# A shorter exponent table, parameter products from PSUM, and a new written-out order in an S4D and gMLP kernel

## The chip, the cores and the metric

The kernel runs on one core of a Trainium2 chip. Its engines are TensorE (PE, with its weight loads shown apart as PEld), VectorE (DVE), ScalarE (ACT), GpSimd (POOL) and SyncE (SP, which here only issues DMAs). Each has its own in-order queue; they meet through semaphores. The metric is the device time of one execution in microseconds, lower is better; the median of several runs counts.

## What is computed

The reference, cut to what matters. `A_u` is 2048 x 512, there are 128 modes for each of the 512 channels, and the mixer is 1792 wide.

```python
def _A_ref(u, log_A_real, A_imag, C_real, C_imag, log_dt, D_skip):
    dt = jnp.exp(log_dt)
    A = -jnp.exp(log_A_real) + 1j * A_imag
    C = (C_real + 1j * C_imag) * dt[:, None]
    P = jnp.exp((A * dt[:, None])[:, :, None] * pos[None, None, :])
    K = 2.0 * jnp.einsum("dn,dnl->dl", C, P).real
    y = jnp.fft.irfft(jnp.fft.rfft(u_t, L2) * jnp.fft.rfft(K, L2)[None], L2)[:, :, :L]
    return y + u * D_skip[None, None, :]
def _B_ref(x, w_in, w_sp, b_sp, w_out):
    z = _gelu(jnp.einsum("bsd,df->bsf", x, w_in))
    z1 = z[..., :Fh]
    z2 = _layernorm(z[..., Fh:], axis=-1)
    g = jnp.einsum("ts,bsf->btf", w_sp, z2) + b_sp[None, :, None]
    return jnp.einsum("bsf,fd->bsd", z1 * g, w_out)
h = x + _A_ref(_layernorm(x, axis=-1), ...)
h2 = h + _B_ref(_layernorm(h, axis=-1), ...)
```

## The kernel before

**Phase A** (`phase_a`, line 268) makes the long convolution. The channels are cut into 4 chunks of 8 units each. A unit (`unit`, line 483) builds a piece of the kernel K: its exponentials come from a table `mt` of short rows of powers, which `table` (line 473) makes once for each half chunk, eight tables in all. POOL multiplies the rates by the list `c_lt` in three instructions, ACT takes one Exp over the whole table, and POOL multiplies the weights into the last four columns. Each unit then makes three 128x512 factors by POOL, each the product of eight entries of one part of the row with four of another (lines 498 to 501); ACT makes sines from phases in PSUM, DVE multiplies, and TensorE contracts.

`params` (line 405) turns the complex weights C into modulus, phase and real part, for chunk 0, chunk 1, and chunks 2 and 3 together. Its last steps multiply the sine and cosine of an angle (`si`, `co`) by the smaller and the larger part (`mn`, `mx`) and add them, on POOL (lines 459 to 461), before ACT, TensorE and a copy bring the result to `rcs`, which the table's last multiply reads. `norm_x` (line 366) normalises x ahead of its transform: DVE takes statistics and writes part of the result, and 64 column scalings fill the rest, each on ACT or on POOL.

The transforms are pieces: A and B for x, C and D for K, E for the inverse. D multiplies the two spectra; in the last chunk three of its eight groups go through an ACT copy and two POOL multiplies each (lines 608 to 612) and the others through one DVE multiply. `piece_e` writes `big`, from which the next phase reads.

All of phase A is first recorded and then issued in an order that is written out by hand, as three strings. `RANKS` (line 37) holds a rank for each recorded operation, two digits each: the sorted ranks are the order on all five queues. `FORMS` says for each choice (`either`) which engine takes it: evacuations of PSUM on ACT or DVE, column scalings on ACT or POOL. `BANKS` gives each PSUM tile one of five banks. The instructions of this phase all carry line 252, the line that issues them.

**Phase B1** (`phase_b1`, line 700) finishes the inverse and makes z1. `lines(n, g, g+1)` (line 748) is TensorE's last stage for a quarter n of the positions, into PSUM tiles `y`, of which there are seven. `put_by` (line 764) copies a tile to `stash` by two ACT copies of 64 partitions, `add` (line 770) adds x to it on DVE, `moments` takes its statistics and stores h, `centre` forms the mean over partitions by TensorE (`lnh_pm`) and the squares, `spread` does the same for the variance (`lnh_pv`), and `root` takes the inverse root. `by_halves` and `transposed` scale, transpose and split the result into two parts `ht`, and `column` multiplies it by the weights (`pz`), takes the gelu on ACT and stores z1. The order is that of the calls from line 889 on, on every engine but SP.

**Phases B2 and B3** make z2, the spatial product and the output projection; they are not touched.

Of the kernel before, what the change touches and what calls it, by code (L numbers as in the profile page):

```python
# [23 lines left out]
NCH = 4  # L24
# [47 lines left out]
def constants():  # L72
# [40 lines left out]
    for i in range(8):  # L113
# [12 lines left out]
    c["c_lt"] = np.broadcast_to(-lt, (P, 34))  # L126
# [141 lines left out]
def phase_a(ctx, gen, tc, ins, cst, ident, c_mean, c_inv, Q, wp, scr):  # L268
# [8 lines left out]
    def one(pool, tag, shape, dt=F32):  # L277
        return pool.tile([P] + shape, dt, tag=tag, name=tag)
# [9 lines left out]
    c_lt, c_f, dpad, half_pi, magic, dummy, dts, ndt, dt2 = (wb(n) for n in (34, 256, P, 1, 1, 1, NCH, NCH, NCH))  # L288
# [3 lines left out]
    mts = [one(g1, f"mt{h}", [64, 34]) for h in range(2)]  # L292
# [112 lines left out]
    def params(al, c0, n, rt):  # L405
# [13 lines left out]
        si = ai  # L419
# [19 lines left out]
        nc.scalar.activation(co, a, AF.Sin, bias=half_pi)  # L439
# [260 lines left out]
def phase_b1(tc, es, right, left, rest, c_mean, mhalf, qt, ins, cst, wp, scr):  # L700
# [69 lines left out]
    def add(n, g):  # L770
        v = xqs[n % 3][:, 4 * g:4 * g + 4, :]
        nc.vector.tensor_add(v, stash[n][:, g].rearrange("p (l x) -> p l x", l=4), v)  # L772
# [114 lines left out]
    with tc.manual_schedule(engines={E.PE, E.DVE, E.Activation, E.Pool}):  # L887
# [7 lines left out]
        nc.scalar.activation(stats[:, 1, 0, 0:1], mhalf, AF.Gelu_apprx_tanh)
# [400 lines left out]
```

## Time and profile before

| | |
|---|---|
| median of 3 runs | 819.7 us (815.72 to 820.77) |
| profiled execution | 819.86 us, its span 818.1 us |
| TensorE busy | 766.9 us, 94% of the span |
| DVE, ACT, POOL busy | 592.3, 456.3 and 308.5 us |
| mean granted TensorE clock | 0.992 |
| phase A, to the first `y` matmul | 274.87 us |
| first `pz` matmul of z1 | 297.28 us |

A row of the view by groups reads: line, engine, operation, output <- inputs, shapes, count, then busy time and mean time of one in ns, then the idle time of the engine just before these instructions and what ended most of it. A row of the timeline reads: start, length, engine, line, operation, names, shapes, count, and in brackets the idle time before it and what ended it. A row of the view by stretches gives the stretch, then the busy time and number of instructions of PE, PEld, DVE, ACT and POOL, the granted clock, the share of the DMA engines, and GB/s.

### The profile page before, as it was taken

What the parts mean: (1) busy time and instruction counts of PE and PEld (TensorE: products, weight loads), DVE (VectorE), ACT (ScalarE), POOL (GpSimd) and SP (SyncE); (2) the same over time, 40 slices, a digit from 0 to 9 for tenths busy, and PEclk for the clock granted to TensorE, in tenths of its full rate; (3) what the DMA queues carried; (4) which work ended last, traced back from release to release, by engine and by line L of the source; (5) the groups of instructions that cost most, each with busy time, mean ns of one, the idle gap of its engine ahead of it and who ended that gap; (6) DMA issues with size and microseconds to landing.
All of it is one profiled execution on the core that took longest, in us unless ns stands there. A gap on an engine that the chain in (4) does not pass through costs nothing.

```text
span 818.1 us, 20010 instructions
## 1 busy us (share of the span) xinstructions
PE 766.9 (94%) x8081; PEld 652.2 (80%) x8081; DVE 592.3 (72%) x1153; ACT 456.3 (56%) x813; POOL 308.5 (38%) x356
## 2 busy tenths in 40 slices
PE   2489999999988889999999999999999999999998
PEld 1267889889978787888999888888888888888887
DVE  8998987967763468642677799978849883887534
ACT  8999989788653575553233355575345442454111
POOL 8999999978456100000331101233220002231200
PEclk9999999999998999999999999999999999999999
DMA  7604514415049146552361146999798449799642
GB/s 262 205 14 154 119 51 108 102 51 115 2 106 397 63 104 169 143 192 97 96 139 49 65 122 173 204 225 237 180 229 203 151 124 190 165 252 249 140 114 79
DMA packets 65004, 119.48 MB, mean 146 GB/s; under 512 B 6800, under 2 KB 21264, under 8 KB 63632
## 3 DMA queue, kind: packets, MB, share of 16 engines
q1 hardware_dynamic: 53248, 96.71, 39.5%
q0 software_dynamic: 11664, 21.50, 15.8%
q8 instruction: 63, 1.03, 0.5%
q14 instruction: 29, 0.24, 0.1%
HBM read 90.40 MB, written 19.40 MB: 134 GB/s over the span
## 4 chain that ended last, share of the span: by engine, by line
PE 61%; DVE 1%; ACT 1%; issue 0%
PE m L1183 34%; PE pz L978 9%; PE pz L876 8%; PE po L1106 7%; PE pl L1106 2%; DVE stats L776 0%; ACT ht L833 0%; ACT w1r L824 0%; DVE w1r L831 0%; DVE xq L772 0%; ACT stash L768 0%; DVE ht L837 0%; PE lnh_pm L785 0%; PE lnh_pv L799 0%; ACT zo L879 0%
## 5 line engine op out<-in xcount | busy, mean ns | idle before, releaser
L1183 PE MATMUL m<-wts,zc_wa 128*128 128x512 f32 x700 | 221.0, 395 | 0.0
L1183 PEld LDWEIGHTS m<-wts,zc_wa 128*128 128x128 f32 x700 | 131.7, 188 | 31.0
L1054 POOL DMA_DIRECT2D raws<-in_w_sp_dram x64 | 58.2, 1016 | 213.4 <-DMA raws<-in_w_sp_dram 206.3
L1183 PE MATMUL m<-wts,zc_wb 128*128 128x512 f32 x350 | 138.0, 394 | 0.0
L252 POOL TENSOR_TENSOR wa<-mt 128x512 f32<-128x512 f32 x96 | 106.7, 1130 | 12.1 <-DVE big L252 4.2
L690 ACT CAST wts<-raws 128x512 fp32r<-128x512 f32 x112 | 69.1, 619 | 51.3 <-PE m L1183 26.2
L691 DVE TENSOR_TENSOR wts<-raws,wts 128x512 fp32r<-128x512 f32 x112 | 76.4, 685 | 15.5 <-ACT wts L690 15.5
L1183 PEld LDWEIGHTS m<-wts,zc_wb 128*128 128x128 f32 x350 | 65.8, 188 | 15.6
L978 PE MATMUL pz<-w,ht 128*128 128x448 f32 x384 | 77.0, 362 | 0.0
L876 PE MATMUL pz<-ht,w1h 128*128 128x512 f32 (+1 forms) x248 | 73.8, 377 | 2.9 <-ACT ht L833 2.6
L978 PEld LDWEIGHTS pz<-w,ht 128*128 128x128 f32 x384 | 72.0, 188 | 4.9
L984 POOL TENSOR_SCALAR sm<-sm 128x1 f32<-128x1 f32 x16 | 5.6, 347 | 165.0 <-DVE sm L983 165.0
L252 PE MATMUL ps<-c_inv,trio 128*128 128x128 f32 x512 | 60.8, 277 | 1.9 <-DVE trio L252 1.4
L1106 PE MATMUL po<-w,gz 128*128 128x512 f32 x252 | 61.7, 392 | 0.0
L252 PEld LDWEIGHTS ps<-c_inv,trio 128*128 128x128 f32 x512 | 58.5, 192 | 3.3 <-POOL trio L252 1.6
L690 ACT CAST zc_wa<-raws 128x384 fp32r<-128x384 f32 (+1 forms) x70 | 37.1, 533 | 41.5 <-DVE raws L1088 21.5
L252 PE MATMUL ps<-big,a 128*128 128x128 f32 x448 | 57.4, 285 | 1.2 <-ACT big L252 0.7
L252 DVE TENSOR_TENSOR f<-ps,wa 128x512 f32<-128x512 f32 (+1 forms) x64 | 46.9, 750 | 14.2 <-ACT ps L252 12.5
L252 PEld LDWEIGHTS ps<-big,a 128*128 128x128 f32 x448 | 53.8, 197 | 3.7 <-DVE trio L252 0.9
L1106 PEld LDWEIGHTS po<-w,gz 128*128 128x128 f32 x252 | 47.3, 188 | 10.7
L876 PEld LDWEIGHTS pz<-ht,w1h 128*128 128x128 f32 x248 | 45.1, 188 | 12.8 <-ACT ht L833 3.5
L690 ACT CAST zc_wa<-z 128x128 fp32r<-128x128 f32 (+2 forms) x56 | 23.7, 431 | 45.6 <-PE m L1183 38.7
(157 smaller groups left out, 1463.0 us busy)
## 6 DMA issues: line engine op xcount, KB each, us to landing
raws<-in_w_sp_dram SPq DMA_DIRECT2D x112, 256.0 KB, 4.1
raws<-in_w_sp_dram POOLq DMA_DIRECT2D x80, 256.0 KB, 6.0
trio<-trio SPq DMA_DIRECT2D x32, 256.0 KB, 4.3
scr_z<-zo SPq DMA_DIRECT2D x28, 256.0 KB, 2.1
big<-in_u_a_dram SPq DMA_DIRECT2D x8, 512.0 KB, 6.1
xq<-in_u_b_dram SPq DMA_DIRECT2D x4, 1024.0 KB, 9.0
g<-in_c_g_dram SPq DMA_DIRECT2D x4, 1024.0 KB, 9.1
scr_h<-xq SPq DMA_DIRECT2D x16, 256.0 KB, 4.1
```

The lines of the kernel that those rows point to most:

```text
L252: r = getattr(getattr(self.nc, e), method)(*map(self.real, args), **{k: self.real(x) for k, x in kw.items()})
L690: nc.scalar.copy(hi, src)
L691: (engine or nc.vector).tensor_tensor(lo, src, hi.bitcast(F32), op=ALU.subtract)
L876: nc.tensor.matmul(pt[:, w], a[:, q, f], ht[n][k][:, q, w], start=((q, i) == terms[0]), stop=((q, i) == terms[-1]))
L978: nc.tensor.matmul(pt[:, :FQ], a[:, q], w2[:, b, q, f], start=(q == 0 and i == 0), stop=(q == 3 and i == 2))
L984: nc.gpsimd.tensor_scalar_add(sm[:, 14:15], sm[:, 13:14], 1e-5)
L1054: nc.gpsimd.dma_start(r, ws[1], accum_op=ALU.add)
L1106: nc.tensor.matmul(pt, gz[fb][x][:, P * a:P * a + P], wo[:, y, fb, w], start=(first and fb == fbs[0] and i == 0), stop=(last and fb == fbs ...
L1183: nc.tensor.matmul(pt, x[:, f], y, start=(k == 0 and i == 0), stop=(k == KT - 1 and i == 2))
```

## The change

The list behind the table has 27 entries for 34: the part that held 7 to 0 is gone, and the unit reads the part 0 to 7 backwards in its place; 0 to 448 by steps of 64 is one part of eight. In `params`, `si` and the cosine `cp` are PSUM tiles, and DVE makes their products and the sum; six more PSUM tiles are to be placed. All three strings are new. Between the inverse and z1, the first two groups of quarter 0 are not put by: DVE adds them to x straight from PSUM, in two halves each. The adds and statistics go in pairs, `lines(2, 0, 1)` stands before `centre(0)`, and the root of quarter 0 before `lines(2, 2, 3)`.

```diff
     lt = np.concatenate([
-        24 - 8 * np.arange(4), 1 + np.arange(7), 7 - np.arange(8), 64 * (1 + np.arange(7)),
-        32 + 8 * np.arange(4), 512 * np.arange(4),
+        24 - 8 * np.arange(4), 1 + np.arange(7), 64 * np.arange(8), 32 + 8 * np.arange(4), 512 * np.arange(4),
     ]).astype(f8)
...
-        si = ai
+        si, cp = bank("si", [P, N]), bank("co", [P, N])
...
-        nc.scalar.activation(co, a, AF.Sin, bias=half_pi)
+        nc.scalar.activation(cp, a, AF.Sin, bias=half_pi)
...
-        nc.gpsimd.tensor_tensor(co, co, mx, op=ALU.mult)
-        nc.gpsimd.tensor_tensor(si, si, mn, op=ALU.mult)
-        nc.gpsimd.tensor_tensor(co, co, si, op=ALU.add)
+        nc.vector.tensor_mul(co, cp, mx)
+        nc.vector.tensor_mul(si, si, mn)
+        nc.vector.tensor_add(co, si, co)
...
-        nc.gpsimd.tensor_tensor(mv[:, :, :, 30:], mv[:, :, :, 30:], w.unsqueeze(3).to_broadcast([P, 8, 8, 4]), op=ALU.mult)
+        nc.gpsimd.tensor_tensor(mv[:, :, :, 23:], mv[:, :, :, 23:], w.unsqueeze(3).to_broadcast([P, 8, 8, 4]), op=ALU.mult)
...
-        for i, (a0, b0) in ((2, (18, 30)), (0, (3, 26)), (1, (11, 0))):
-            ta = mt[:, d0:d0 + 16, a0:a0 + 8].unsqueeze(2).to_broadcast([P, 16, 4, 8])
+        for i, (a, b0) in ((2, (slice(11, 19), 23)), (0, (slice(3, 11), 19)), (1, (slice(10, 2, -1), 0))):
+            ta = mt[:, d0:d0 + 16, a].unsqueeze(2).to_broadcast([P, 16, 4, 8])
...
     def add(n, g):
         v = xqs[n % 3][:, 4 * g:4 * g + 4, :]
-        nc.vector.tensor_add(v, stash[n][:, g].rearrange("p (l x) -> p l x", l=4), v)
+        if n == 0 and g < 2:
+            y = ys[n, g].rearrange("p l (x d) -> p l d x", d=4)
+            v = xqs[0][64 * g:64 * g + 64, :8].rearrange("p l (d x) -> p l d x", d=4)
+            for odd in range(2):
+                nc.vector.tensor_add(v[:, odd::2], y[64 * odd:64 * odd + 64], v[:, odd::2])
+        else:
+            nc.vector.tensor_add(v, stash[n][:, g].rearrange("p (l x) -> p l x", l=4), v)
...
-        for n in range(2):
-            for g in range(4):
-                put_by(n, g)
+        put_by(0, 2)
+        put_by(0, 3)
+        for g in range(4):
+            put_by(1, g)
         nc.scalar.activation(stats[:, 1, 0, 0:1], mhalf, AF.Gelu_apprx_tanh)
-        for g in range(4):
+        for g in range(0, 4, 2):
             add(0, g)
+            add(0, g + 1)
             moments(0, g)
+            moments(0, g + 1)
+        lines(2, 0, 1)
         centre(0)
-        lines(2, 0, 1)
         add(1, 0)
+        root(0, spread(0))
         lines(2, 2, 3)
-        root(0, spread(0))
         put_by(2, 0)
         put_by(2, 1)
```

The three strings differ in nearly every entry and are left out here; what they say of the order is told where it is used.

More of the change, by code (lines that the diff above doesn't have):

```diff
@@ L58 @@
-    "JeI4I6IMI1I2IIIcI3IJI5ILINIWIdIfIzI-JIJXI+J4JFJ5J7J8JRJPJJJQJLJMJNJSJTJUJYJZJaIOIiInI8IgIhIwIqJAJ0J1J6JBJCJDJEJKJbJcJuJw"
-    "JfJgJhJrJkJpJjJmJqJnJiJoJlJxJ+JzJyJ-JsJtKCKEK2K9K6KFK3KAK0K1K7K8K4K5KBKD"
+    "01000H0g290N0Z181A1P1a1k1l1h470+6W0a02030B270k2g060708090A0C0E0F0I0P0R0U0b0i0G0l1J0u1C0J1213151E1F1K0D0L0K0Q0S0V0T0d0e0f"
+    "0m0n0-16171G1T1U1j1V1b1Q1S1m1s1t1v0t0h0y1X1u1w0M05040O0o1W0z0r0p2D101R2C2A1M110q2H2e4V5P2o1H2q464N0j0c0X0Y0w0x0W1r0s1B1x"
+    "1-1D140v1I1y1i1+1q1N1L191p1c1f1O1n1d1g2120222E2G2J2K2V2L2M2W2Y2d2h2i2s2v2x2y2+3134333v3f3w3W3T3k3y4E3t3K3L433x3E4W3J3j3l"
@@ new lines @@
+    "623I4Q3G4C3b6C353R5J404B593F4D3B382O24373Y263P2B2t393S3O323Q2F2R3C282P2N2p2Q3e2U3H2n3N2a2-2c3d2X363g3h3i3m3r4T3s3u3-4448"
+    "4H4J4L4R4X4Z4d4h4o4i4p4s534q4w644v5E4t5b5s685x506j5+5z6z5r5-5A5S6S5p5H6f6r5O5Y5C6y54716s6l7G757i7zAN1Y1Z1o2Z2l2m2u3M1e1z"
+    "23252I2SGn2T2f2b2z3A3n3p4I4O4Y4u5D2r4-4a5V6J6Y6n8P2w3D3c4r5F5W4F4x4e4c5T5U606k6t5i5k5j5l5m5nHS696M6F6O6g6o6p6+6-707H7J7o"
+    "AZ7v907n8IAgB6BJBg6G6N6b7g8d8gB3CpCq61635R5X6H6I5f5g6K6L5G5Q5o5q5y666m6u898A7l807O7c6q736X6a7m866d6e8i8r304M2j3V3z45494A"
@@ new lines @@
+    "4g4b4y4l4z52878o8q3Z3U2k3X3a3o3q414G424S4K4U4f888J8K4P51564j4k4+5Z5a5d5c655e6A6D6T7p7q3+4m4n5557585B5K5M5L5h5N5u5w7T8z92"
+    "7I817f5I7a7s8H6777795t5v6E6x76787A7M7P7X7b9M9U9V6R6Z6B6P6Q6c6U6V6i6h6w6v7D7E7Q8+8-7k8F7y7+7-858C8D8G8E8U8S8m8s8t9J9K7Y7K"
+    "7N7L7Z7j7F7R7U7S8M7V8N8O999I9LAE8l7r9dA4A6AI8Q8R7W7d7t7u7w7x7e7h727483847B7C8e8f9495ATAU9l9o8p8v9z9+AXAh9N9P9mA59Y9g9u9v"
+    "AJAKAOAPACADAbAn9-A3C7CRBTBdCMCcBRBSCoCrBWBxAuAyAwB5DLDM8L978n8j8k8x988y919R9C969O9D9W9f9nBuC88Z8X8V828B8T8u8b8a8c8Y8W93"
@@ new lines @@
+    "8w9A9E9wAlAq9Z9h9q9Q9c9i9p9x9r9y9k9sA1A2A9AACXD0D28h9B9S9F9G9H9T9j9e9t9X9aA09bA7ABBCBmBtBaBPBLBnBUBvB-AdALAVAFAGAHBAAMAi"
+    "AfAQAWB4BKBMBNCEDUDfAmAzA8AjAkArB1AvAsB7A-AtB0B2B8BEBlChCiA+BZBjBIBVBcBzC9BpCFBiBkCJCACPCdCfD1D4BDBOBYBFBGBHBXBqBeByBQBb"
+    "BfBhC1C2CeCyCzCjC3CgDQDtDuENASAYAaARAeAcAoApB9AxBBBrBoBwCWBsB+CBCvCwE0CCCDDxDGDHDeDjDADBE8EBDbDcDVDoE9EEDEDFDqDsEUEaDgDr"
+    "DhDyE7EFEcEdEGEYE6ECGRGWFVFWGUGfEwE+GQGXFUFhFiFqFIFJGVHcCGCVCQCZCaCbClC-CmD7CnCkD8C+DJDKEhFbFxC0C4C5C6CHCICNCSCLCTCOCKCU"
@@ new lines @@
+    "CYCtCxDSFYFZDCDPDTDNDODXDkDYDiDwDlDmDnDpDzD+D-ESEeCsCuDID3D5D6DDDRD9DWDZDaDvDdE1E2FpGdGmFXFaEXF1EDFSFTEOELEAE3E4E5EHEVEP"
+    "ElEMEIEkEWEmEoG3H8HOEZEtEiEbEfEgF0ExEpEyEuEqF6F3FCFDFyG4GDEsEvFKF2F5F7FeFAFBFsF8FMFrFkFzF-GbHCHDE-FFFPF4FGFHFvFRFLFlFNFQ"
+    "FuFwG8G9GFGeGtHAGgHdGxGMHgH+EJEQEKERETEjF9FOFEEnErEzFfFgFnFcFoFdGiGjG0G1HEHLHxHyGuGvHsHtHFHVHGHeI6IDGwH5HzI4HmHwHkHlHoHv"
+    "H-I8HnHuHPHfHbHrIMIQI9IEIOIdIiInIAIBILIRIqIyIPIfJYJZFtF+G7FjG2G5GSGNGAGOG6GCGcGTGkGlIsIxJ4FmGBGEGGGHGIGaGKGJGLGYGPG-GhH2"
@@ L60 @@
+    "H4J5J6J7GZGpGoGqGrGsH6H7GzHNG+GyHMHBHWHpHqJNJOH0H9H3H1HHHIHXHTHKHUHQHJHRHYHZHaI3J9JAI0HiHjI5ICIFIZISIHITINIGIWIaIbIuIzI+"
+    "J8IIHhIJI1I2I7IcIgIKImIXIUIYIhItJPJVJWJXIVIvIpIeIjIkI-IoIlJ1IwIrJBJ0JKJLJdJeJfJDJIJEJ2J3JCJHJQJFJRJJJGJSJMJTJUJaJbJcJnJo"
+    "JgJhJrJiJsJtJlJmJyJ-JpJqJjJkJ+JzJwJxJuJvK8KAK3K9K2KBK6K7KEKFKCKDK4K5K0K1"
 )
 FORMS = (
-    "000000001010100011000011100100000101100000011000001000000111001100110000100000000000100111100001010101101111101000000001"
-    "00000110110110010100000100100100001110010100000010000001000110001101001101100000000101101110001001100000111001101111"
+    "000000000011100110101010101011010000101001001000110111001101001110100011101000001000011000100100010100000100011111000000"
@@ L64 @@
+    "00000011010001000101110111101011100100000101010101011010010101111101001000010010001010101000011001110100000001101011"
 )
 BANKS = (
-    "414220313014444030432220022044434342124120412142014001422000123112321121011031223434430243400423134324420430131103321432"
-    "034214411300222000123324434132420203334344321432242224410132113203001432002102101211314313432104023143234243141003422442"
-    "030104322301034014314303413333144024"
+    "421123440400211334443433310202101124431134224211421042214022402042214110302201001124433033402433414403033414410430132223"
@@ L69 @@
+    "011421213103311240021020111332040242104433432434432340214123210331143003421331224020021220434431434211300343212301113104"
+    "411340232010300042233021313434433404313424"
 )
@@ L287, in phase_a @@
     cs_bufs = [wb(2 * W).rearrange("p (k a w) -> p k a w", k=2, a=2) for _ in range(2)]
-    c_lt, c_f, dpad, half_pi, magic, dummy, dts, ndt, dt2 = (wb(n) for n in (34, 256, P, 1, 1, 1, NCH, NCH, NCH))
+    c_lt, c_f, dpad, half_pi, magic, dummy, dts, ndt, dt2 = (wb(n) for n in (27, 256, P, 1, 1, 1, NCH, NCH, NCH))
     c_k = one(g1, "c_k", [2, W], F32R)
@@ L291, in phase_a @@
     sws = [one(g1, f"sw{h}", [4, 2, NS]) for h in range(2)]
-    mts = [one(g1, f"mt{h}", [64, 34]) for h in range(2)]
+    mts = [one(g1, f"mt{h}", [64, 27]) for h in range(2)]
     f_bufs = [one(g1, f"f{i}", [4, W]) for i in range(3)]
```

26 lines of the change are left out of this document (3 added, 23 removed).

## The prediction

> **What bounds the kernel now.** I read first the chain of work that ended last, then the time by stretches, then the groups of instructions by shape, and last the timeline at three places that the change touches.
>
> ```profile
> 321.49 5.38 PE pz L876 x22
> ```
>
> The columns are start, length and what ran. From here on the chain has nothing but TensorE until the last 4 us or so: whatever the change saves must be saved before that, and is then kept to the end.
>
> ```profile
> 0.00:40.00 40.00, 12.99 (x94) 8.63 (x95) 35.12 (x152) 35.58 (x83) 36.25 (x47) 1.00 0.73 239
> 40.00:80.00 40.00, 34.45 (x1045) 27.02 (x1045) 35.49 (x49) 38.50 (x71) 38.64 (x48) 1.00 0.27 86
> 80.00:160.00 80.00, 78.49 (x1935) 70.01 (x1938) 68.51 (x91) 73.17 (x106) 78.00 (x81) 1.00 0.41 97
> 160.00:240.00 80.00, 78.52 (x1780) 71.91 (x1773) 56.30 (x73) 59.32 (x81) 55.17 (x60) 1.00 0.25 57
> 240.00:275.00 35.00, 29.74 (x388) 28.52 (x392) 13.90 (x17) 8.94 (x14) 16.71 (x12) 0.85 0.72 264
> 275.00:300.00 25.00, 20.16 (x543) 19.20 (x543) 13.81 (x48) 18.23 (x32) 0.00 (x0) 0.93 0.35 87
> ```
>
> The columns after the stretch are PE, weight loads, DVE, ACT, POOL, the granted clock. Up to 40 us PE is starved and the three others are about 90% busy. From 40 to 160 us POOL is 97% busy (116.64 of 120 us) and ACT 93%; from 160 to 240 us POOL and ACT have some 20 us to spare and PE is the bound. From 240 to 300 us every engine has gaps: that is the tail of the transforms and the way to the first z1 product, and there a wait is worth its full length.
>
> **The change, part by part.**
>
> ```profile
> L252 POOL TENSOR_TENSOR mt<-wb 128x816 f32<-128x816 f32 x16 | 25.6, 1606 | 1.4 <-ACT trio L252 1.3
> L252 POOL TENSOR_TENSOR mt<-wb 128x544 f32<-128x544 f32 x8 | 9.0, 1130 | 0.0
> L252 ACT ACTIVATE mt<-mt 128x2176 f32<-128x2176 f32 x8 | 16.0, 2017 | 0.1
> L252 ACT ACT_TABLE_LOAD x16 | 20.5, 1283 | 2.7 <-PE ps L252 1.1 <-PEq L1290 0.7 <-DVE big L252 0.7
> L252 POOL TENSOR_TENSOR trio<-trio 128x128 f32<-128x128 f32 x12 | 5.3, 451 | 0.3
> L252 POOL TENSOR_TENSOR big<-big 128x256 f32<-128x256 f32 x6 | 4.2, 704 | 0.4 <-ACT big L252 0.4
> L252 DVE TENSOR_TENSOR trio<-trio,ps 128x128 f32<-128x128 f32 x2 | 0.6, 284 | 0.0
> L252 POOL TENSOR_TENSOR wa<-mt 128x512 f32<-128x512 f32 x96 | 106.7, 1130 | 12.1 <-DVE big L252 4.2 <-ACT mt L252 3.9 <-PE ps L252 2.3
> L252 DVE TENSOR_TENSOR trio<-ps,trio 128x1024 f32<-128x1024 f32 x29 | 34.2, 1217 | 7.4 <-PE ps L252 6.9
> L252 DVE TENSOR_TENSOR f<-ps,wa 128x512 f32<-128x512 f32 x56 | 37.4, 684 | 11.2 <-ACT ps L252 9.5 <-POOL ks L252 1.3 <-POOL wa L252 0.2
> ```
>
> *Table of 27.* Each of 8 tables is three POOL multiplies and one Exp. POOL's two shapes give (1606-1130)/272 = 1.75 ns an element; 448 elements fewer are 0.78 us a table, 6.3 us in all. Exp by proportion (2017 x 7/34) saves 0.4 us each, 3.3 us.
>
> *Falling powers read backwards.* One of a unit's three 128x512 multiplies reads its short factor with a negative step. No row has one. The 96 of a unit take 1130 ns with their several strides; two plain POOL operands take 451 and 704 ns for 128 and 256 elements, which would be 1210 ns for 512. So between -2.6 and +2.6 us for 32 of them (0.08 us each way); I take 0, by the 96, which are this instruction. POOL being the bound up to 160 us, either end would show.
>
> *Parameter products from PSUM.* Nine multiplies and adds leave POOL: 6 x 0.451 + 3 x 0.704 = 4.8 us. On DVE they are 6 x 0.284 + 3 x about 0.42 (my estimate, scaled by the step from 128 to 256 elements that POOL shows) = 3.0 us, in stretches where DVE is 88% busy.
>
> *New order.* The three strings give each engine's order outright, so I compared the two orders entry by entry. Of the free choices, nine column scalings go from ACT to POOL, the net of the PSUM evacuations moves four 128x512 copies from ACT to DVE, and two 128x256 copies go back to ACT.
>
> ```profile
> 0.73 3.90 POOL L252 MEMSET sw<- 32x1024 f32 x4 [0.29 <-POOLq L1290]
> 5.91 4.24 POOL L252 TENSOR_TENSOR mt<-wb 128x816 f32<-128x816 f32 x3 [1.27 <-ACT trio L252]
> 7.43 0.26 ACT L252 ACTIVATE ps<-ps 128x128 f32<-128x128 f32 x1 [0.24 <-DVE ps L252]
> 7.71 1.28 ACT L252 ACT_TABLE_LOAD   x1
> 9.00 0.37 ACT L252 ACTIVATE trio<-ps,wb 128x128 f32<-128x128 f32 x1
> 23.94 2.34 ACT L252 ACTIVATE big<-big,trio 128x96 f32<-128x96 f32 x6
> 28.90 3.48 POOL L252 TENSOR_SCALAR big<-big,trio 128x96 f32<-128x96 f32 x5
> ```
>
> A column scaling costs ACT 2.34/6 = 0.39 us and POOL 3.48/5 = 0.70 us: +6.3 us for POOL, -3.5 us for ACT. POOL's sum is -6.3 - 4.8 + 6.3 = -4.8 us; DVE's is +3.0 and four copies of about 0.68 less two small ones, +5 us.
>
> Table loads: I counted switches between the function sets of Exp, Arctan and Sin along ACT's order. A dummy Sin now stands ahead of the first Arctan, which saves one; tables 0.0 and 0.1, and 2.0 and 2.1, no longer share an Exp stretch, which adds four: 19 for 16, +3 x 1.283 = +3.8 us. ACT's sum is -3.3 + 3.8 - 3.5 and about -2 for copies, -5 us. A load is followed at once by the next activation (7.71 + 1.28, then 9.00). The Trainium skill, ScalarE: Activation LUTs, What ACT_TABLE_LOAD costs, adds some 1380 ns of drain to each switch; by it three loads would be 8.0 us and ACT's sum near -1, but the rows here show no drain.
>
> The start speaks against the change. POOL now multiplies its first table at 5.91 us with 2.0 us idle before. In the new order the copy of the rates that it waits for stands on ACT behind the table load for Sin, Arctan, two Sines and an Abs; SP also issues the list for the table behind two blocks of u and c_inv. From 7.43 us, four 0.3 us steps and the copy put that start near 8.9 us, with only two memsets (1.95 us) ahead: 6.9 us idle, 4.9 more. Against POOL's -4.8 that is nothing saved by the end of the stream, and by units 18 and 19, where POOL's sum is only 4.0 less, 0.9 lost. I take +0.5 us for everything up to 240 us; between -4.8 (the idle start is covered) and the price of the slow rival below. SP's other moves (stack loads earlier, later block loads) feed work that is behind POOL's queue here. What is queued on DVE behind the nine new operations is the x normalisation, which feeds the first transforms; I hold that to be inside the 0.5.
>
> ```profile
> 248.20 8.24 PE L252 MATMUL ps<-big,a 128*128 128x128 f32 x56 [0.70 <-ACT big L252]
> 253.57 6.20 POOL L252 TENSOR_TENSOR trio<-trio 128x512 f32<-128x512 f32 x5 [1.28 <-ACT trio L252]
> 259.50 14.65 PE L252 MATMUL ps<-c_inv,trio 128*128 128x128 f32 x128 [1.41 <-DVE trio L252]
> ```
>
> *Last spectrum product (D3).* Three of its eight groups go by an ACT copy to six POOL multiplies of 1.24 us. Now the second copy comes after another group, and POOL waits 1.28 us. In the new order the three copied groups come first, so the six run without that wait. DVE is last next: its first group is there after four of PE (8 matmuls each, 14.65/128 = 0.114 us apart, 3.7 us), and five products of 1.22 us end at 9.8 us, where the inverse now starts 11.3 us after the first matmul: -1.5 us. Bounds: 0 (only two banks alternate now, and the waits stay) to -2.2 (POOL alone sets it: 0.9 for PE, 0.8 for a copy of the 0.6 us kind and its hand-over, 6 x 1.24, so 9.1).
>
> ```profile
> 274.87 7.57 PE L756 MATMUL y<-big,g 64*64 64x128 f32 x256 [0.72 <-ACT big L252]
> 277.00 9.55 ACT L768 COPY stash<-y 64x512 f32<-64x512 f32 x16 [2.18 <-PE y L756]
> 279.40 0.69 DVE L772 TENSOR_TENSOR xq<-stash,xq 128x512 f32<-128x512 f32 x1 [5.65 <-ACT stash L768]
> 280.13 0.87 DVE L776 BATCH_NORM_STATS2 stats<-xq 128x6 f32<-128x128 f32 x4
> 285.55 0.68 PE L785 MATMUL lnh_pm<-stats,c_mean 128*128 128x16 f32 x4 [3.11 <-DVE stats L776]
> 286.15 5.28 PE L756 MATMUL y<-big,g 64*64 64x128 f32 x128
> 286.57 1.28 ACT L895 ACT_TABLE_LOAD   x1
> 291.36 0.62 PE L799 MATMUL lnh_pv<-small,c_mean 128*128 128x16 f32 x4
> 291.91 3.72 PE L756 MATMUL y<-big,g 64*64 64x128 f32 x128
> 292.02 0.17 DVE L804 TENSOR_SCALAR small<-lnh_pv 128x16 f32<-128x16 f32 x1 [4.39 <-PE lnh_pv L799]
> 294.00 1.37 DVE L822 TENSOR_SCALAR w1r<-xq,small 128x128 f32<-128x128 f32 x5
> 297.28 0.39 PE L876 MATMUL pz<-ht,w1h 128*128 128x256 f32 x1 [1.65 <-ACT ht L833]
> ```
>
> *Between inverse and z1*, against the same start at 274.87. DVE is idle twice: 5.65 us for ACT's copies, and 4.39 us because the second mean (lnh_pv) stands on PE's queue behind the 5.28 us of lines(2). The change takes both. DVE adds the first two groups from PSUM itself at 277.0: four adds of 64 partitions, about 0.65 us each (the `f<-ps,wa` row, back to back), to 279.6; eight statistics 1.74, to 281.35; two adds, their copies being done at 281.2, to 282.8; eight statistics, to 284.5, where it was 285.5. lines(2,0,1) now fills PE's 3.11 us wait, and lines(2,2,3) comes after lnh_pv, so pm, the four centre steps and pv follow each other: pv at 286.1 to 286.7, root to 288.65, for 294.00 now. ACT ends later than DVE: 12 copies of 0.597 us from 278.75 to 286.0, the table load and its use to 287.5, four copies of lines(2) to 289.9. Its share of the scaling starts there; now it starts with DVE's, about 294.1. So the first product comes 4.3 us earlier, at 293.0. Bounds: -5.35 (DVE alone) and -3.4: the 128 matmuls of lines took 5.28 us once and 3.72 us the next time, the first after the 3.11 us gap with a granted clock below 1 in that stretch; if all of lines(3) runs at the slower rate, PE is free for the product only at 293.8. I take -4.3, the faster rate, because the gap ahead of them is filled. The Trainium skill, TensorE: Matmul & The Clock Gate, The HAM clock gate, has one idle window of about 3.4 us halve the clock; by that too the clock would stay whole.
>
> The profiled execution took 819.9 us (span 818.1 and 1.8 around it), the median of the runs shown is 819.7, so no correction: 819.9 - 4.3 - 1.5 + 0.5 = **814.6 us**.
>
> **The rivals.**
> *Faster: POOL's saving arrives whole.* The late first table is covered, since units 0 to 3 need less of POOL's queue ahead of them in the new order. Then -4.8 in place of +0.5: 809.3 us. For it: 97% POOL up to 160 us. Against it: PE is the bound after that.
> *No change: the gain behind the inverse is given back.* The scaling waits for ACT behind its copies, and the columns' second half, which has its own ACT and DVE queue, starts when it does today; only DVE's first 0.9 us remain: 819.9 - 0.9 - 1.5 + 0.5 = 818.0 us.
> *Slower: DVE becomes the bound of the middle.* It gets 5 us more, and the new order puts all eight 1.22 us products of the second spectrum ahead of unit 21, where four stood behind unit 20: another 4.9. If DVE has no slack there, the stream comes 9.9 us later: 819.9 - 5.8 + 9.9 = 824.0 us. For it: DVE is 88% busy in the first 80 us. Against it: it idles 11.5 us from 80 to 160 us and 23.7 us after. It decides once those 11.5 us cannot take in the 9.9.
>
> **How the numbers follow.** My forecast has 0.50, the faster rival 0.19, no change 0.17, the slower 0.14. One per cent, 8.2 us, is about what a measurement of this kernel can tell from no change; the bounds are 811.5 and 827.9. Faster by over 1%: the faster rival and a fifth of the forecast's spread, 0.29. Slower: the upper third of the slow rival, 0.05. The same: 0.66. The forecast alone spans its bounds, 811 to 818 us. The range goes from 806 (both ends of the two late terms with POOL's whole saving, 819.9 - 5.35 - 2.2 - 4.8 = 807.5, and a little) to 824.
>
> **What would show it.** Lines(2,0,1) before lnh_pm; lnh_pv within 2 us of lnh_pm; the root within 14 us of the first y matmul, for 17.2 now; the first pz 18.1 us after it, for 22.4; inverse 9.8 us after the last spectrum product begins, for 11.3; 19 table loads ahead of the gelu's; the 128x648 and 128x432 table multiplies near 1.31 and 0.93 us; POOL's first one near 8.9 us; the first y matmul at 273.9, for 274.87. A first y matmul before 270 or after 279 would show the order of the stream mis-sized; a backward read above 1.15 us, that term.

## The result and the profile after

The changed kernel takes 831.9 us (median; 829.2 to 833.7), the kernel before 820.2 in the same rounds: a ratio of 1.0142, with an interval of 1.0103 to 1.0182. It is 1.4% slower, outside the predicted range. The profiled execution took 833.7 us, its span is 831.9. Executions of one kernel differ with the granted clock: the kernel before took 814.7 to 816.2 us in those that had all of it, and 824.3 to 825.3 in those that had 0.984.

First the same view by stretches as before (after the stretch: its length, then PE, weight loads, DVE, ACT, POOL, the granted clock):

```profile
0.00:40.00 40.00, 11.39 (x59) 7.47 (x61) 32.83 (x144) 30.35 (x69) 28.92 (x38) 1.00 0.56 177
40.00:80.00 40.00, 31.52 (x818) 24.18 (x810) 34.16 (x57) 36.06 (x74) 39.08 (x51) 0.91 0.42 140
80.00:160.00 80.00, 74.69 (x1919) 65.31 (x1919) 60.64 (x81) 62.87 (x86) 62.67 (x68) 0.97 0.38 89
160.00:240.00 80.00, 78.74 (x1666) 72.39 (x1666) 62.57 (x81) 62.38 (x84) 59.88 (x63) 0.99 0.23 55
240.00:293.00 53.00, 45.38 (x779) 42.38 (x777) 23.34 (x30) 20.72 (x33) 26.18 (x25) 0.90 0.58 195
```

The three other engines have more room than before (POOL 62.67 of 80 us from 80 to 160 us, where it had 78.00), and yet the stream is late. TensorE has 818 rows from 40 to 80 us where it had 1045, and its clock, which was whole up to 240 us, is not in any stretch from 40 us on. Next the way from the first y product to the first pz, on TensorE and VectorE:

```profile
293.49 5.97 PE L755 MATMUL y<-big,g 64*64 64x128 f32 x209 [0.83 <-issue]
302.93 0.62 PE L790 MATMUL lnh_pm<-stats,c_mean 128*128 128x16 f32 x4
304.40 0.62 PE L804 MATMUL lnh_pv<-small,c_mean 128*128 128x16 f32 x4 [0.86 <-DVE small L798]
304.95 3.93 PE L755 MATMUL y<-big,g 64*64 64x128 f32 x133
311.25 0.39 PE L881 MATMUL pz<-ht,w1h 128*128 128x256 f32 x1
```

```profile
295.49 2.83 DVE L775 TENSOR_TENSOR xq<-y,xq 64x512 f32<-64x512 f32 x4 [2.10 <-PE y L755]
307.04 1.36 DVE L827 TENSOR_SCALAR w1r<-xq,small 128x128 f32<-128x128 f32 x5
```

This part gained: first y to first pz is 17.76 us, and was 22.41. But the first y comes at 293.49 us, and came at 274.87. So 18.6 us are lost ahead of y, and 4.65 won behind it. What was to be gained on GpSimd is there too (groups by shape):

```profile
L251 POOL TENSOR_TENSOR wa<-mt 128x512 f32<-128x512 f32 x96 | 104.9, 1106 | 20.9 <-PE ps L251 9.3 <-DVE f L251 6.4 <-ACT mt L251 3.8
L251 ACT ACT_TABLE_LOAD x19 | 24.4, 1283 | 6.2 <-DVE big L251 4.9 <-PEq L1298 0.7 <-PE ps L251 0.4
L251 POOL TENSOR_TENSOR mt<-wb 128x648 f32<-128x648 f32 x16 | 21.1, 1323 | 0.0
L251 POOL TENSOR_TENSOR mt<-wb 128x432 f32<-128x432 f32 x8 | 7.5, 943 | 7.4 <-ACT wb L251 7.4
```

**Where TensorE stands.** In the timeline of the changed kernel TensorE stops in the middle of one group of matmuls, with no operand to wait for:

```profile
75.39 0.68 PE L251 MATMUL ps<-wb,big 64*64 64x64 f32 x29 [0.53 <-ACT ks L251]
78.64 0.33 PE L251 MATMUL ps<-wb,big 64*64 64x64 f32 x3 [2.57 <-issue]
```

29 of 32 matmuls, 2.57 us of nothing, then the last three. "Issue" means that it waited for nothing the profile shows. The page's list of transfer queues has one more clue, a queue of instructions, and the same list by windows shows when it moved (columns: packets, MB, share of the 16 engines). Whole span:

```profile
q8 instruction: 63, 1.03, 0.5%
```

From 71.9 to 76.1 us, and then from 76.1 to 78.6 us:

```profile
q1 hardware_dynamic: 369, 1.50, 97.1%
```

```profile
q1 hardware_dynamic: 444, 0.30, 50.0%
q8 instruction: 1, 0.02, 2.2%
```

For 4 us the transfer engines are full of data and no instructions come; then one packet of 16 KB comes, and TensorE goes on. 1.03 MB in 63 packets are 16 KB each. How much of TensorE's program that is shows in the count of rows between the four longest stops (one stretch ends in each; a row is a weight load and a matmul):

```profile
0.00:77.00 77.00, 41.55 (x855) 30.35 (x855) 66.00 (x198) 63.49 (x140) 65.00 (x84) 0.96 0.50 163
77.00:104.00 27.00, 23.16 (x638) 19.30 (x639) 17.61 (x24) 21.06 (x29) 19.20 (x23) 0.94 0.46 102
104.00:156.50 52.50, 49.86 (x1270) 44.38 (x1270) 43.33 (x57) 43.32 (x58) 45.34 (x49) 1.00 0.29 71
156.50:260.50 104.00, 98.41 (x2163) 90.22 (x2162) 77.78 (x101) 75.50 (x105) 73.12 (x79) 0.98 0.32 72
```

638, 1270 and 2163 rows are 5, 10 and 17 blocks of 127.2, some 254 instructions. All nine such stops before y stand a whole number of blocks apart, and each ends 1.2 to 1.7 us after an instruction packet has landed. The whole program of 8081 rows is 63.5 such blocks, and the queue has 63 packets. The stops sum to 10.6 us; the kernel before has two, of 0.7 us together. Behind the stops of 2.57 and 1.93 us the clock falls (granted clock third from the end):

```profile
79.60:83.00 3.40, 3.40 (x49) 3.17 (x51) 1.23 (x2) 0.34 (x2) 2.26 (x3) 0.50 0.02 5
158.10:161.50 3.40, 3.40 (x19) 3.40 (x17) 0.70 (x2) 1.28 (x2) 0.00 (x0) 0.50 0.96 201
```

The Trainium skill, Runtime: NRT & Kernel Launch, Instruction fetch mechanics, says that instructions come in blocks of 16 KiB, 256 of them, the next while the current one runs, and that crossing a border is mostly hidden. The size agrees (16 KB a packet, 127.2 rows); that it is hidden holds in the kernel before (0.7 us) and not here (10.6 us).

### The profile page after: what moved, and what is told of

Its sections match the earlier page's. It is cut to its first block, busy times and chain, and to the rows that moved or that the text cites. A ratio compares the mean times of both kernels' runs of the same rounds, so it can differ in the third digit from the quotient of the medians.

```text
span 831.9 us, 19990 instructions
## 1 busy us (share of the span) xinstructions
PE 773.2 (93%) x8081; PEld 656.7 (79%) x8081; DVE 598.2 (72%) x1167; ACT 449.4 (54%) x800; POOL 302.4 (36%) x356
## 3 DMA queue, kind: packets, MB, share of 16 engines
q8 instruction: 63, 1.03, 0.5%
## 4 chain that ended last, share of the span: by engine, by line
PE 83%; DVE 5%; ACT 5%; DMA 3%; issue 3%; POOL 1%; SPq 1%; DVEq 0%; ACTq 0%; POOLq 0%
PE m L1191 33%; PE ps L251 22%; PE pz L986 9%; PE pz L881 7%; PE po L1114 7%; PE pl L1114 2%; DMA big<-in_u_a_dram 1%; DMA w1r<-in_w_dram 1%; ACT ps L251 1%; DVE trio L251 1%; ACT big L251 1%; PE y L755 1%; DVE f L251 1%; POOL wa L251 1%; DVE ps L251 0%
## 5 line engine op out<-in xcount | busy, mean ns | idle before, releaser
L251 POOL TENSOR_TENSOR wa<-mt 128x512 f32<-128x512 f32 x96 | 104.9, 1106 | 20.9 <-PE ps L251 9.3
L251 PE MATMUL ps<-big,a 128*128 128x128 f32 x448 | 60.4, 293 | 1.5 <-ACT big L251 0.7
L1114 PE MATMUL po<-w,gz 128*128 128x512 f32 x252 | 61.7, 392 | 0.0
L251 PE MATMUL ps<-c_inv,trio 128*128 128x128 f32 x512 | 60.1, 277 | 1.5 <-DVE trio L251 1.4
L251 PEld LDWEIGHTS ps<-big,a 128*128 128x128 f32 x448 | 56.4, 204 | 4.4 <-DVE trio L251 1.8
L1114 PEld LDWEIGHTS po<-w,gz 128*128 128x128 f32 x252 | 47.3, 188 | 10.7
L251 DVE COPY big<-ps 128x512 f32<-128x512 f32 x47 | 31.4, 685 | 24.9 <-PE ps L251 24.7
```

What stands on the lines that cost most here:

```text
L251: r = getattr(getattr(self.nc, e), method)(*map(self.real, args), **{k: self.real(x) for k, x in kw.items()})
L1114: nc.tensor.matmul(pt, gz[fb][x][:, P * a:P * a + P], wo[:, y, fb, w], start=(first and fb == fbs[0] and i == 0), stop=(last and fb == fbs ...
```

## The experiments

All runs beside each other. Time and ratio are medians; the columns behind them come from the one profiled execution of each kernel. "Last x" is the end of the copy of the last transform of x, D0 and D2 the end of the last product of spectra of chunks 0 and 2 (the recorded expectations call them channels; the rows matched to the orders entry by entry), "stops" the stops of 0.2 us and more at block borders before the first y, "half" the half-clock stretches that begin after 40 us and before y. Times in us.

| run | time | ratio (95%) | last x | D0 | D2 | stops | half | first y |
|---|---|---|---|---|---|---|---|---|
| before | 818.9 to 820.3 | 1 | 57.4 | 115.9 | 216.5 | 0.7 | 10.2 | 274.9 |
| changed | 831.9 | 1.010 to 1.018 | 62.3 | 123.3 | 233.3 | 10.6 | 23.9 | 293.5 |
| b1_alone | 812.8 | 0.986 to 0.992 | 57.4 | 115.8 | 216.3 | 0.8 | 3.4 | 272.2 |
| old_order | 814.0 | 0.986 to 0.993 | 57.2 | 115.3 | 215.9 | 0.0 | 10.2 | 274.3 |
| before_s64 | 825.0 | 1.002 to 1.009 | 63.0 | 121.3 | 221.8 | 0.6 | 10.2 | 280.6 |
| before_h24 | 823.9 | 1.002 to 1.008 | 57.3 | 119.8 | 222.3 | 6.2 | 6.8 | 279.2 |
| after_s64 | 841.9 | 1.019 to 1.029 | 75.4 | 136.6 | 246.9 | 9.9 | 20.5 | 304.2 |
| after_h48 | 825.4 | 1.003 to 1.010 | 64.4 | 120.6 | 225.9 | 4.7 | 10.2 | 282.9 |
| thin_exchange | 829.5 | 1.006 to 1.016 | 61.7 | 120.7 | 230.2 | 7.6 | 23.9 | 290.4 |
| start_old | 829.3 | 1.008 to 1.016 | 60.1 | 123.3 | 231.3 | 6.3 | 13.7 | 288.4 |
| start_new | 827.2 | 1.007 to 1.015 | 61.8 | 130.7 | 231.5 | 2.9 | 13.7 | 286.4 |
| u_first | 832.5 | 1.014 to 1.019 | 63.4 | 127.8 | 235.7 | 10.2 | 17.1 | 293.1 |
| pool_first | 825.5 | 1.005 to 1.011 | 60.8 | 118.9 | 228.3 | 8.7 | 13.7 | 286.0 |
| both_h48 | 823.2 | 1.004 to 1.009 | 64.2 | 120.7 | 225.2 | 4.1 | 10.2 | 282.6 |
| pool_h48 | 823.3 | 1.001 to 1.007 | 62.8 | 118.1 | 222.7 | 4.4 | 10.2 | 282.9 |
| params_dve | 819.0 | 0.995 to 1.002 | 61.1 | 120.8 | 221.3 | 0.5 | 6.8 | 277.9 |

**Parts alone.** First the part behind y, in the kernel before:

```diff
 def phase_b1(...):   # of the changed kernel; all else as before
+            if n == 0 and g < 2: ...  # adds from PSUM
+        put_by(0, 2); put_by(0, 3); ...  # the new order
```

> The kernel before with only the lines and adds between inverse and z1 in their new order. Theory (that part works as priced, the loss is all in the stream ahead of the inverse): first y matmul where it was, near 274.9 us, first pz 17.8 to 18.1 us after it, time 815 to 816. Rival (the part only gains where the stream comes late, since the loads of g and of the z weights have then landed): first pz 20 us or more after the first y, time 818 to 820.

First y to first pz took 18.18 us: 0.1 above the theory's 17.8 to 18.1 and far from the rival's 20. The first y came at 272.2 and not near 274.9, and the time of 812.8 is 2 us below the theory's range, since its half-clock stretch at 241 us was 3.41 us and not 10.24. TensorE's program up to there is that of before, so nothing in the edit explains that, though all four executions had 0.998 or 1.000 of the clock.

```diff
-    c["c_lt"] = np.broadcast_to(-lt, (P, 34))
+    c["c_lt"] = np.broadcast_to(-lt, (P, 27))
...
-        for i, (a0, b0) in ((2, (18, 30)), (0, (3, 26)), (1, (11, 0))):
+        for i, (a, b0) in ((2, (slice(11, 19), 23)), (0, (slice(3, 11), 19)), (1, (slice(10, 2, -1), 0))):
```

> As b1_alone, and the exponent table of 27 and the falling powers read backwards too, but with the three strings and the parameter products of before. Theory (the table is a gain for GpSimd and the loss is in the order): first y matmul at 270 to 275 us, time 811 to 816. Rival (the smaller table or the backward read is what costs): first y at 280 us or later, time over 820.

First y at 274.34, 814.0: the theory's ranges. The table and the backward read cost nothing. They gain nothing either: old_order is not faster than b1_alone (the intervals cover each other), though GpSimd has 6 us less to do.

**Borders of blocks.** Products of the identity ahead in TensorE's program move every later border:

```diff
             nc.issue(o)
+            seen += o["calls"][0][0] == "tensor"
+            if seen == 3 and o["calls"][0][0] == "tensor":
+                for _ in range(64):
+                    tc.nc.tensor.matmul(nc.banks[0][0:64, 1, 0:64], ident[0:64, 0:64], ident[0:64, 0:64], ...)
```

> The changed kernel with 64 more 64x64 TensorE products of the identity behind its first three transposes, where TensorE waits some 4 us; they shift the program of TensorE by half a block of instructions and change nothing else. Theory (instruction blocks: TensorE stops where the next 256 instructions have not come, because the transfer of the block stood behind data; 10.6 us of such stops before the first y): the stops at 76, 103, 155 and 260 us go, others of fewer us appear 64 matmuls earlier in the program, and the time moves by several us, to 820 to 829. Rival (the stops are waits of the new order): the same stops at the same matmuls, time 831 to 834.

> The kernel before with the same 64 products behind its first three transposes. Theory (instruction blocks; the kernel before has its block borders where data transfers leave them room, 0.7 us of such stops in all): new stops, first y 2 to 8 us later, time 822 to 828. Rival (the stops belong to the new order): no change beyond the products themselves, 819.5 to 821.5.

after_s64 missed both sides' numbers, and before_s64 has the theory's time for another reason (no new stops, 0.6 us in all). The edit did not do what it was for: 64 products are 128 rows, a whole block, so the borders stayed at the same matmuls. They also hold TensorE for 13.9 us, as the first row of after_s64 shows; the second is the stop that was at 76 us, again behind 29 of 32:

```profile
10.40 13.91 PE L678 MATMUL ps<-ident 64*64 64x64 f32 x128
...
90.95 0.47 PE L251 MATMUL ps<-wb,big 64*64 64x64 f32 x3 [2.29 <-issue]
```

They tell something else. before_s64 has its last transform of x 5.7 us late, D0 5.4, D2 5.3 and y 5.7: **what is lost at the start is handed on almost whole.** In after_s64 13.1 us become 10.7 at y.

Then 48 products (96 rows, three quarters of a block) in the changed kernel, and 24 in the kernel before, spread over four quarters of the array:

> The changed kernel with 48 more 64x64 products of the identity in a pause of TensorE near 11 us (96 rows in its record, spread over four quarters of the array so that they take some 2 us of the 3.4 us pause). The 64 products of after_s64 were 128 rows, a whole block, so borders of blocks stayed at the same matmuls; 96 rows move each border by three quarters of a block. Theory (instruction blocks): the long stops at rows 855, 1493, 2763 and 4926 go, the sum of such stops before the first y falls from 10.6 us to 1 to 5, and with the half-clock stretches behind them the first y comes at 280 to 287 us; time 818 to 826. Rival (waits of the new order that only look like block stops): the same stops ahead of the same matmuls, first y 293 to 296, time 831 to 834.

> The kernel before with 24 such products (48 rows) in its pause of 5.6 us near 7 us. Theory (instruction blocks; the order of before has few stops by where its borders fall): new stops of 4 to 10 us in all, first y at 278 to 286, time 823 to 831. Rival: no stops over 1 us in all, first y 274 to 276, time 819 to 822.

Both came as the block theory said, and the rivals fell. One of the new stops of before_h24, again in the middle of one group:

```profile
73.62 0.53 PE L252 MATMUL ps<-f 128*32 128x64 f32 x19 [1.67 <-issue]
```

In after_h48 the first y is 10.6 us earlier, though the products themselves put the start back by 2. Its rows by stretches, each ending in a stop:

```profile
0.00:62.30 62.30, 29.84 (x601) 21.58 (x601) 51.47 (x175) 49.40 (x111) 49.20 (x64) 0.73 0.48 154
62.30:88.00 25.70, 23.20 (x637) 19.30 (x637) 23.25 (x36) 22.66 (x39) 23.09 (x30) 1.00 0.40 128
88.00:102.50 14.50, 12.99 (x383) 10.59 (x383) 10.64 (x16) 12.39 (x19) 13.02 (x15) 1.00 0.77 172
102.50:248.50 146.00, 143.16 (x3306) 130.53 (x3306) 115.71 (x152) 117.12 (x159) 116.17 (x124) 1.00 0.30 70
```

637, 383 and 3306 are 5, 3 and 26 blocks: the stops keep to the borders and leave the matmuls. From 102.5 to 248.5 us there is none, and TensorE is busy 98%: from the last transform of x to D2 this run needs 161.6 us, before 159.1, the changed kernel 171.0. So the new order of the middle costs little by itself; nearly all of its 11.9 us more are stops and the slow clock behind them. The sum closes: between its last x and D2 the changed kernel has 8.5 us of stops and two half-clock stretches of 3.41 us; if these cost half their length, that is 11.9 us, where before has 0.3. Taken off in the same way (half-clock time only outside the stops), 158.0 to 159.3 us are left in all thirteen kernels that have one of the two orders from start to D2 (some with a few entries moved or with the products added), whose measured 158.7 to 172.2 us differ by 13.5; start_old, start_new and params_dve, whose orders were put together anew, keep 161.5, 163.4 and 160.2. And the order of before was spared by where its borders fell: moved by 48 rows it has 6.2 us of stops.

That data holds the blocks up was tried by thinning a transfer:

```diff
-                    nc.sync.dma_start(b[o:o + 64, d:d + 8], a[i:i + 64, d:d + 8])
+                    w = 1 if c == 0 else 8
+                    nc.sync.dma_start(b[o:o + 64, d:d + w], a[i:i + 64, d:d + w])
```

> The changed kernel in which the eight transfers that swap the two halves of channel 0's spectrum move one eighth of their columns, so that the first product of spectra works in part on what stood there. TensorE's program and all orders are those of the changed kernel. Theory (the stop at row 855 is a block of instructions queued behind these 2 MB): that stop falls from 2.57 us to under 0.5, the half-clock stretch at 79.6 us goes, the stops at rows 1493, 2763 and 4926 stay; first y 288.5 to 291, time 827 to 830. Rival (a block comes late for a reason other than the data on the queues): the stop at row 855 stays, first y 293 to 294, time 831 to 834.

The time and y lie in the theory's ranges, but by luck, since the place was wrong: the stop at row 855 stayed (2.29 us). The swap does not run there; from 71 to 75 us the queues carry other transfers and are as full as in the changed kernel. It runs from 92 to 104 us, and the stops there went or shrank, the one at row 1493 among them, which was to stay. The time is loose, too: the four executions took 822.0 to 831.6 us. Changed kernel, stretch and timeline, then the same of thin_exchange:

```profile
100.00:104.00 4.00, 2.77 (x97) 2.41 (x97) 1.15 (x2) 3.71 (x5) 4.00 (x5) 1.00 0.99 221
```

```profile
104.28 0.32 PE L251 MATMUL ps<-f 128*32 128x64 f32 x8 [1.51 <-issue]
```

```profile
99.00:103.00 4.00, 3.63 (x114) 2.81 (x103) 2.50 (x4) 3.48 (x5) 4.00 (x6) 1.00 0.05 9
```

```profile
101.48 0.32 PE L251 MATMUL ps<-f 128*32 128x64 f32 x8 [0.37 <-issue]
```

The same border at the same matmul: with the transfer engines 99% busy it costs 1.51 us, with 5% it costs 0.37. The one of 0.78 us before it (98 us) is gone.

**The start.** The first 430 of 1296 entries of one order with the rest of the other (Sine and cosine of the parameters in SBUF in both):

> The changed kernel with the first 430 entries of the order (the parameters of channel 0, the x normalisation, the first tables, units 0 to 3 in part, up to some 60 us) from before and the rest as changed; Sine and cosine of the parameters stand in SBUF for that. Theory (the late start is 5 of the 18.6 us and is handed on in full, as the 13.8 us of after_s64 were): last transform of x some 5 us earlier than in the changed kernel, near 57.5 us, first y 286 to 290, time 824 to 829. Rival (later engines catch the start up): first y 292 to 295, time 830 to 834.

> The other half: the first 430 entries from the changed order, the rest as before, with the table of 27, the parameter products on VectorE and the new lines and adds. Theory (late start handed on): against old_order (814.0) 5 us more, first y 277 to 281, time 817 to 821. Rival (start is caught up, the whole loss is in the later order): first y 272 to 275, time 812 to 815.

start_old gave the y forecast, but its last x came at 60.1 and not 57.5, and its time lies 0.3 us above the range. start_new missed by 6 us: at the seam it lost 10 us more, with a stop of 2.58 us at a border and 13.7 us of half clock; from D0 on (130.7, 14.8 late) the old order handed on just that (15.0 late at D2). Neither tells the start's parts apart; two more kernels were to, which move entries of the order alone. In u_first SyncE issues the last three blocks of u and c_mean ahead of the parameters of chunk 1. In pool_first it issues c_lt ahead of u, and the transpose and ACT copy of the rates of chunk 0 come ahead of Arctan.

> The changed kernel with the last three blocks of u and the list c_mean issued by SyncE ahead of the parameters of channel 1, which make SyncE wait until 12 us; nothing else moved. Theory (the start loses through the x normalisation: VectorE stands 1.59 us at a statistic of the second half whose u lands at 19.8 us, and the chain of the first half's means is queued behind it): no such stand, last transform of x 1.5 to 2 us earlier, at 60.3 to 60.8 us, first y 291.2 to 292.2, time 829 to 831. Rival (the start loses through GpSimd's late first table): first y 293 to 294, time 831 to 833.

> The changed kernel with the list for the exponent table loaded ahead of u, and the transpose and ScalarE copy of the rates of channel 0 ahead of Arctan, so that GpSimd's first table multiply comes at 6.3 to 7.5 us instead of 9.94. The prediction's own term (GpSimd bounds the stream up to 160 us, its idle start is paid in full): first y 2.5 to 3.5 us earlier, 290 to 291, time 828 to 830. Rival (GpSimd has room in the first 80 us, the normalisation of x sets the first transform): first y 293 to 294, time 831 to 833.

u_first missed the theory; its y and time are the rival's, but not for the rival's reason. The u are early now, but the parameters that they passed are late, and ScalarE, in its order, stands 3.65 us for them:

```profile
18.39 0.31 ACT L252 ACTIVATE trio<-trio 128x128 f32<-128x128 f32 x1 [3.65 <-DMA trio<-in_par_dram]
```

pool_first gained more than either side said. GpSimd's first multiply in the changed kernel, and in pool_first:

```profile
9.94 4.78 POOL L251 TENSOR_TENSOR mt<-wb 128x432 f32<-128x432 f32 x4 [7.38 <-ACT wb L251]
```

```profile
6.99 4.78 POOL L252 TENSOR_TENSOR mt<-wb 128x432 f32<-128x432 f32 x4 [4.43 <-ACT wb L252]
```

2.95 us earlier there are 1.5 at the last x, 4.4 at D0 and 5.0 at D2. What is gained between last x and D0 is again stops (4.2 us there, for 5.5 in the changed kernel) and the half-clock stretch of 79.6 us, which is gone; the other 2.5 of the 7.5 at y come with a half-clock stretch at 256 us of 3.41 us instead of 10.24. So more than half of the gain is not GpSimd's start itself.

> The changed kernel with both of these moves and the 48 products of after_h48. Theory (block stops and the normalisation of x, terms that add): against after_h48 (first y 282.9, 825.4 us) 1.5 to 2 us less: first y 280.9 to 281.5, time 822 to 825. Rival (GpSimd's start counts as well): first y 278 to 279, time 819 to 822. A third way: the borders fall elsewhere among the transfers again, 285 or more.

> pool_first with the 48 products of after_h48. Theory (GpSimd's late start and the block stops are two separate losses, so both gains add; both_h48 lost its part through the earlier u): first y 277.5 to 280, time 817.5 to 821. Rival (the two are one, each only shifts the borders among the transfers): first y 282 to 286, time 822 to 826.

Neither added up as the theory said, though the time of both_h48 lies in its range; in pool_h48 y and time are the rival's. In both_h48 the last x comes 1.4 us later than in pool_h48, which lacks only u_first's move. In pool_h48 D2 comes 3.3 us earlier than in after_h48, and then a half-clock stretch of 10.24 us at 250 us, where after_h48 had 3.41, takes the same away: a gain ahead of a pause of TensorE is kept only as the clock behind it allows.

> old_order with one more part of the change: the nine parameter products go from GpSimd to VectorE, at their places in the order of before, each add right behind its second product; Sine and cosine stand in SBUF. The prediction's term (GpSimd -4.8 us, VectorE +3.0, in sum inside 0.5): last transform of x at 57 to 58 us as in old_order (57.21), first y 273 to 275.5, time 812 to 815. Rival (VectorE stands in order at ScalarE's Sine with the statistics of x queued behind it, which is why start_old had its last transform of x at 60.12 us with the old start): 59.5 to 60.5 us, first y 276 to 278, time 815.5 to 818.

The rival had the side: 61.1, 277.9 and 819.0, with last x and time beyond even its range. Its reason covers only a part: the product behind Sine took 1.29 us there, with both operands in SBUF, and VectorE had waited 0.89 us for it; with an operand in PSUM, as changed, it took 0.28 without a wait. These 1.9 us are half of the 3.9 by which the last x is later than in old_order; the rest was not found, and why the product took 1.29 us is not shown (GpSimd was in its table multiplies, from 6.19 to 13.20 us). Nor is it the price of the changed kernel, which has no such wait:

```profile
9.83 1.29 DVE L252 TENSOR_TENSOR trio<-trio 128x128 f32<-128x128 f32 x1 [0.89 <-ACT trio L252]
```

```profile
9.43 0.28 DVE L251 TENSOR_TENSOR trio<-ps,trio 128x128 f32<-128x128 f32 x1
```

**A version that beats both** is b1_alone, at 0.986 to 0.992 of the kernel before; old_order equals it. At an equal granted clock the gain is smaller, about 3 us: 812.0 and 812.5 us with all of it, where before took 814.7 to 816.2, and 813.1 and 813.3 at 0.998, for 816.0 to 817.3. The rest of the 7 us is that its executions had more of the clock, and no run shows that the edit brings that.

## Why the prediction was wrong

- *Between inverse and z1 (-4.3 us).* Right in its steps. pv follows pm by 1.47 us (within 2), the scaling behind the root starts 13.55 us after the first y (14 forecast for the root), first pz after 17.76 us (18.1). b1_alone shows it without the rest, at 18.18. One step had luck: the forecast took the whole clock because the gap ahead of lines(2) is filled. The changed kernel and b1_alone have it there, but old_order and pool_h48, with the same order of the lines, have 3.41 us of half clock at 286.0 and 294.7 us and their first pz after 18.40 and 18.53.
- *"I take +0.5 us for everything up to 240 us."* This is the step that failed. D2 ends 16.8 us later. The term set sums of work per engine against each other with GpSimd as the bound; old_order, with GpSimd's queue 6 us shorter and D2 only 0.4 us earlier than in b1_alone, shows that it was not. TensorE was: before, it was busy 157.0 of the 160 us from 80 to 240 us. What holds TensorE up in the changed kernel is the delivery of its own program, which no sum of busy times shows: 4.9 us are lost by the last transform of x, and 11.9 from there to D2, nearly all stops at borders of blocks (8.5 us) and the clock behind them (up to 3.4), as after_h48, before_h24 and thin_exchange bear out.
- *The late first table (4.9 us of idle, set off against GpSimd's -4.8).* The late start came (9.94 us, forecast 8.9). With it mended (pool_first) the last x comes 1.5 us earlier and D2 5.0 us; what lies between the two is mostly shorter stops and one half-clock stretch less. The shorter sum that was to pay for it saves nothing. What else makes the start late was not found: the last x still comes at 60.8 for 57.4.
- *D3 (-1.5 us).* Wrong. From the first product to the inverse it took 12.84 us. The 11.3 of before, which I put down to GpSimd's wait, holds a half-clock stretch. Its start and the inverse behind it, in the changed kernel, in b1_alone (old D3 order) and in after_h48 (new D3 order), the last two at the whole clock (their inverse rows are cut short by the end of the view's window; only the starts count):

```profile
265.29 7.33 PE L251 MATMUL ps<-big,a 128*128 128x128 f32 x40 [0.70 <-ACT big L251]
...
278.13 14.53 PE L251 MATMUL ps<-c_inv,trio 128*128 128x128 f32 x128 [1.41 <-DVE trio L251]
```

```profile
247.16 6.61 PE L252 MATMUL ps<-big,a 128*128 128x128 f32 x56 [0.73 <-ACT big L252]
...
256.83 3.38 PE L252 MATMUL ps<-c_inv,trio 128*128 128x128 f32 x27 [1.41 <-DVE trio L252]
```

```profile
257.27 4.83 PE L251 MATMUL ps<-big,a 128*128 128x128 f32 x40 [0.70 <-ACT big L251]
...
267.57 2.69 PE L251 MATMUL ps<-c_inv,trio 128*128 128x128 f32 x22 [1.41 <-DVE trio L251]
```

  At the whole clock the old order takes 9.67 us and the new one 10.30: it loses 0.6.
- *Table of 27, backward read, loads.* The prices were right: 1.323 and 0.943 us (1.31 and 0.93), 1.106 us for the unit's multiplies (1.130 before, no charge taken), 19 loads. They lie beside TensorE's work.
- *The rivals.* The slow one had the side but not the mechanism: VectorE idles 19.4 us from 80 to 160 us, more than the 11.5 before. The bound that was named (a first y after 279 us shows the stream's order mis-sized) is what came.

Open stays which part of the start besides the late table costs the other 3.4 us, and what makes one half-clock stretch last 3.41 and another 10.24 us. For the first there is a candidate that no run tested alone: the changed kernel has 6.83 us at half clock from 48.9 us, behind a pause of 2.10 us, and before has none there; in thin_exchange that stretch was 3.41 us, and the last x came 0.6 us earlier.

## What to carry to other kernels

Where TensorE is busy 98% of a long stretch, as here, sums of work on the other engines said nothing of the time; ask what can stop TensorE, and count a microsecond lost at the start of the stretch almost in full. A long program of small matmuls (127 here in 4 to 6 us) runs into borders of instruction blocks; a burst of transfers that starts just behind a border held the next block up here, so that two orders of nearly equal work differed by 10 us, and 24 or 48 matmuls more ahead of them moved that either way. Before a stretch's length is read as a wait, look at the granted clock in it.

## What the runs showed of the hardware

TensorE's instructions came in packets of 16 KB, each fetched one block ahead: the packet for a border left some 0.6 to 1.2 us after the border before it where the transfer engines were idle, and 4.2 us after it ahead of the longest stop, where they were full (border at 71.93 us, packet from 76.12 to 77.00, TensorE on from the next border at 78.64). In the changed kernel a pause of TensorE of 2.57 us was followed by 3.41 us at half clock, and one of 1.93 us (156.98) too, but one of 1.51 us (104.28) by none; in pool_first one of 2.02 us (76.39) was followed by none, so the length alone does not decide. All half-clock stretches that began after 40 us lasted 3.41, 6.83 or 10.24 us, one, two or three times the same; the Trainium skill, TensorE: Matmul & The Clock Gate, What's actually happening, speaks of free-running windows of 3413 ns, which agrees in the length. The same section of the Trainium skill asks for at least one idle window, and the pause of 2.57 us was shorter than one.

The clock of 1.00 in the first 40 us of the views is not a reading: the record of the clock begins at 40.2 us in the kernel before and at 42.1 in the changed one. In the kernel before, 32 matmuls of one kind (`ps<-f`) took 1.08 us at 37.67 and 0.65 us at 41.58, so the clock was lower there, too. In after_h48, whose record begins at 13.4 us, it was halved from 16.9 to 44.2 us; with the stretch of 6.83 us at 51.0 that makes the 0.73 of its first row.
